# A second level of the seven-product form inside two of seven half products (batches 3 to 7)

## The chip, the core and the metric

The kernel runs on one core of a Trainium2 chip. The metric is the device time of one execution in microseconds. The core's engines work in parallel, each through its own queue in order: TensorE (PE; its weight loads, PEld, overlap its matmuls), VectorE (DVE), ScalarE (ACT), GpSimd (POOL) and SyncE (SP, which here only issues transfers). Semaphores order the engines among each other.

## The reference

Eight batches of 8 heads; `x` has 512 tokens of 64 per head, `state` 32 slots. Attention runs in both directions and its result, 544 rows of 512 per batch, goes through a feed-forward layer:

```python
scores = scale * np.matmul(x, state.transpose(0, 1, 3, 2))
...
xread = np.matmul(a, state)
...
sread = np.matmul(a2, x)
...
h = x @ w_in
g = h * (1.0 / (1.0 + np.exp(-h)))
return (g @ w_out).astype(np.float32)
```

`w_in` is 512x2048, `w_out` 2048x512. The output is 4352x512 in fp32.

## The kernel before

The order of instructions on each engine is written out by hand; the program keeps it.

**First layer.** Because `xread` is a product with the small state, the kernel multiplies state and `w_in` first (`w1_mms`, line 473; W1 is evicted by ACT and DVE in `w1_out`, lines 160 and 162). For a batch, the first layer is then 16 tiles ("slots" 0 to 15). Tile j takes two matmuls of 512 columns (line 540, `h <- aT, W`) into one of two PSUM banks (`psH`), and ACT's SILU (line 568) takes it from there into `g`. `upto(k)` issues tiles up to number k. The last 32 rows of each batch (`sread`) are gathered as a ninth, smaller batch, with tiles of four 256-column matmuls (line 558).

**Softmax of the next batch.** `scores_t` (line 336, also into the `psH` banks) and `exps_t` make the exponentials, transposed by a DMA (`e <- eT`, line 352). `norm_t(n)` sums them on DVE (line 363), takes the reciprocal (364), multiplies one half on POOL and one on DVE (366), and SP issues the transpose of the result, `aT <- an` (line 370). All first-layer tiles of batch n read `aT`.

**Second layer.** `g` (512 tokens, 2048 deep) times `w_out` (512 columns) is done in the seven-product form: tokens, depth and columns are halved, and class `Unit` (its products in `mm`, line 646) issues seven products instead of eight. One product is 8 steps of depth times 2 token blocks, 16 matmuls of 256 columns. Product 1 uses the first token half of `g`'s first depth half and block B11 of `w_out`; product 7 the sum `sums3` (DVE, line 591), made in place, and the weight sum D3. Products 1, 6 and 5 add up in one PSUM bank, `al` (bank "o1"), read in between by ACT (`keep`). Products 7, 2, 4 and 3 each start anew in bank "o0" (`be`), so each waits until DVE has read the one before. `kept[0]` and `kept[1]` are SBUF copies (DVE, line 162) of products 1 and 7. `sums2`, `sums1` and `sums4` are the other sums of `g`, on DVE, for products 6, 5 and 3. POOL and DVE add the parts into `o_sb` (line 594), and SP stores them.

**Order in a batch.** The loop over slots 5 to 15 (`for j in range(lead, NFT)`) issues a tile and then, through `early(j)`, a few units of products 1 and 7 from the list `todo`; one unit is one step of depth, two matmuls. `sums3` is issued at slots 5 and 9, `norm_t(n)` at slot 9, `sums2` from slot 13. After slot 15 come `group_a` (W1 pieces of a later batch, `scores_t`, and in batches 1, 4 and 6 `sread`), product 2 and its sum, then 6, 4, `group_b` (more W1 pieces), 5 with tile 0 of the next batch behind it, and 3 with tiles 1 to 4 of the next batch between its steps (`leads`). W1 pieces take PSUM banks in turn from four (`bank`, a0 to a3). `spread_x` (DVE) copies rows of x beside ones for `sread`. In batch 7 `place_xm` (DVE) arranges the gathered rows, and the tiles of the ninth batch are issued between the products.

Of the kernel before, what the change touches and what calls it, by code (L numbers as in the profile page):

```python
# [8 lines left out]
FP32 = mybir.dt.float32  # L9
# [9 lines left out]
B = 8  # L19
# [23 lines left out]
def kernel(  # L43
# [22 lines left out]
    opool = ctx.enter_context(tc.tile_pool(name="opool", bufs=1))  # L66
    o1pool = ctx.enter_context(tc.tile_pool(name="o1pool", bufs=1))
    spool = ctx.enter_context(tc.tile_pool(name="spool", bufs=1))
# [21 lines left out]
    w_out_sb = pers.tile([128, NFT, DM], BF16)  # L90
    wt = pers.tile([128, 4, 8, 256], BF16)
    xs = pers.tile([128, B, 128], BF16)
    xmT = pers.tile([128, 2, 4, NS, 4], BF16)
# [502 lines left out]
    def t_weights(which, k0, n, eng=nc.vector):  # L596
        k = ds(k0, n)
        for w in which:
# [6 lines left out]
            else:  # L605
                sub(eng, D4[:, k], B21[:, k], D2[:, k])

    class Unit:
        def __init__(self, b):
            self.b = b  # L610
            self.lo, self.hi = gh[b, 0], None
            self.s1 = spool.tile([128, 8, 256], BF16, tag="s1", name="s1")
            self.s2 = spool.tile([128, 8, 256], BF16, tag="s2", name="s2")
            self.al = psO.tile([128, 2, 256], FP32, tag="o1", name="o")
            self.be = None
            self.o = [
                opool.tile([128, 2, DM], FP32, tag=f"o_sb{i}", name="o_sb") for i in range(2)
            ]
# [40 lines left out]
        def sums2(self, k0, n):  # L659
            k = ds(k0, n)  # L660
            sub(nc.vector, self.s2[:, k], self.hi[:, k, 256:512], self.lo[:, k, 256:512])

        def sums1(self):
            for k0 in (0, 4):
                k = ds(k0, 4)
                add(nc.vector, self.s1[:, k], self.s2[:, k], self.lo[:, k, 0:256])

        def sums4(self):
            for k0 in (0, 4):
                k = ds(k0, 4)  # L670
                sub(nc.vector, self.hi[:, k, 0:256], self.hi[:, k, 0:256], self.s2[:, k])

        def block(self, i, c):
# [7 lines left out]
    def store(b, tt, eng):  # L681
        if b < B:
            if tt < 2:
                o_two[tt] = opool.tile([128, 2, DM], FP32, tag=f"o_sb{tt}", name="o_sb")
            o = o_two[tt % 2][:, tt // 2]
        else:
            o = o1pool.tile([128, DM], FP32, tag="o_one", name="o_sb")
        copy(eng, o[:], outs[tt][:])
        if b < B:
            nc.sync.dma_start(out_re[ds(136 * b, 128), tt, :], o)  # L690
        else:
            nc.sync.dma_start(out_sread[ds(512, 32), ds(4 * tt, 4), :], o[:])


    def sread_out_product():
# [4 lines left out]
        s1, s2 = t8("s1"), t8("s2")  # L700
        u1, u3 = (spool.tile([128, 256], FP32, tag=nm, name=nm) for nm in ("u1", "u3"))
        o = [o1pool.tile([128, DM], FP32, tag=f"o_s{i}", name="o_s") for i in range(2)]
        al = psO.tile([128, 256], FP32, tag="o1", name="o")
# [30 lines left out]
        add(nc.vector, s1[:], s2[:], a11)  # L734
        copy(nc.scalar, u1[:], al[:])
        p4 = product(a22, D4)
        add(nc.vector, u1[:], u1[:], o[1][:, hi])
        sub(nc.vector, s2[:], a12, s2[:])
        add(nc.vector, o[1][:, lo], u1[:], p4[:])
        product(s1, D1, al, False)  # L740
        copy(nc.scalar, u3[:], al[:])
        add(nc.vector, o[1][:, hi], o[1][:, hi], u3[:])
        out(1, 0, 512, nc.sync)
# [163 lines left out]
    for b in range(1, B):  # L907
# [82 lines left out]
        if n == B:  # L990
            upto(NFT * B + 2)
        if b == 1:
# [31 lines left out]
        units(6)  # L1024
        u.keep(nc.scalar, 1, 0)
# [75 lines left out]
```

## Time and profile before

| | us |
|---|---|
| median of 3 runs | 203.26 (203.02 to 203.26) |
| the profiled execution | 202.72 |
| its span | 200.9 |
| PE busy on first-layer tiles (line 540) | 72.7 |
| PE busy on the second layer (line 646) | 109.0 |
| ACT busy on SILU (line 568) | 79.9 |
| POOL busy, all its work | 72.3 |

The span is the time between the first and the last instruction in the profile. A row of the timeline has the start in us from the span's beginning, the duration in us, the engine, the source line, the operation, output and input, the shape and a count; in brackets stands the idle time before it and what ended it. Matmuls overlap at their ends, so the start of the next one tells more of their pace than their durations.

### The profile page before, as it was taken

How to read it: one execution, taken by the hardware profiler on the slowest of the kernel's cores; microseconds unless marked ns; L12 is line 12 of the kernel's file. 1: busy time of each engine (PE TensorE's matmuls, PEld its weight loads, DVE VectorE, ACT ScalarE, POOL GpSimd, SP SyncE). 2: the span in 40 equal slices, each digit the busy share in tenths (PEclk: the TensorE clock that was granted, in tenths of full speed). 3: DMA queues.
4: the chain of work that ended last, by engine and by line, in shares of the span. 5: the costliest groups of instructions: out<-in, count | busy, mean ns of one | idle time of the engine just before them, and what ended most of it. 6: DMA issues, size and time to landing. Idle time of an engine off the chain costs nothing.

```text
span 200.9 us, 4650 instructions
## 1 busy us (share of the span) xinstructions
PE 194.4 (97%) x1912; PEld 130.5 (65%) x1912; DVE 139.3 (69%) x244; ACT 138.3 (69%) x245; POOL 72.3 (36%) x89
## 2 busy tenths in 40 slices
PE   7799999999999999999999999999999999999992
PEld 2444435467766676667766676668666876688881
DVE  2852756989997899388938974779369955872072
ACT  2885657889767887778787957888588167724530
POOL 8674333795535602730373034323202230002200
PEclk9999999999999999999999999999999999999999
DMA  5999999993056995594239912943142005000232
GB/s 193 197 206 207 256 253 353 240 233 86 5 162 181 245 267 111 209 279 90 52 151 200 230 32 55 256 102 30 37 197 55 13 3 209 0 3 0 84 128 104
DMA packets 40821, 28.71 MB, mean 143 GB/s; under 512 B 27360, under 2 KB 37472, under 8 KB 40800
## 3 DMA queue, kind: packets, MB, share of 16 engines
q1 hardware_dynamic: 34592, 20.52, 39.8%
q0 software_dynamic: 5920, 7.64, 18.3%
q8 instruction: 15, 0.25, 0.5%
q10 hardware_dynamic: 288, 0.26, 0.4%
q14 instruction: 6, 0.05, 0.1%
HBM read 17.43 MB, written 8.91 MB: 131 GB/s over the span
## 4 chain that ended last, share of the span: by engine, by line
PE 93%; DMA 4%; DVE 0%; POOL 0%; ACT 0%; issue 0%; POOLq 0%
PE o L646 43%; PE h L540 27%; PE ps_w L473 5%; DMA w_in_sb<-in_moe_w_in_dram 4%; PE h L558 4%; PE o L577 3%; PE o_a L577 3%; PE o_s L709 2%; PE o L709 1%; PE ps_sr L420 1%; PE ps_scT L336 1%; PE ps_busy L168 1%; PE h L522 1%; PE ps_xt L257 1%; PE ps_at L402 1%; PE ps_sc L310 0%
## 5 line engine op out<-in xcount | busy, mean ns | idle before, releaser
L568 ACT ACTIVATE g<-h 128x512 bf16<-128x512 f32 (+1 forms) x142 | 79.9, 573 | 34.5 <-PE h L540 23.7
L646 PEld LDWEIGHTS <-g 128*128 128x128 bf16 x560 | 54.2, 98 | 29.2 <-issue 0.5
L540 PE MATMUL h<-aT,W 128*128 128x512 bf16 x252 | 72.7, 379 | 0.2 <-ACT W L160 0.2
L646 PE MATMUL o<-w_out_sb,g 128*128 128x256 bf16 x336 | 48.6, 273 | 0.0
L646 PE MATMUL o<-wt,g 128*128 128x256 bf16 x224 | 33.0, 273 | 0.0
L594 POOL TENSOR_TENSOR o_sb<-o_sb,kept 128x512 f32<-128x512 f32 x7 | 11.0, 1568 | 54.8 <-ACT o_sb L160 39.6
L540 PEld LDWEIGHTS <-W 128*128 128x128 bf16 x252 | 24.4, 98 | 8.7 <-issue 0.9
L646 PE MATMUL o<-wt,s 128*128 128x256 bf16 x224 | 27.4, 273 | 0.0
L594 DVE TENSOR_TENSOR o_sb<-o_sb,o 128x512 f32<-128x512 f32 x14 | 9.6, 683 | 23.9 <-PE o L646 20.5
L162 DVE CAST W<-ps_w 128x512 bf16<-128x512 f32 (+1 forms) x35 | 21.8, 666 | 6.1 <-PE ps_w L473 5.9
L646 PEld LDWEIGHTS <-s 128*128 128x128 bf16 x224 | 21.5, 98 | 4.4 <-issue 2.0
L160 ACT ACTIVATE W<-ps_w 128x512 bf16<-128x512 f32 (+1 forms) x31 | 16.4, 583 | 5.3 <-PE ps_w L473 5.2
L591 DVE TENSOR_TENSOR g<-g 128x1024 bf16<-128x1024 bf16 x15 | 11.6, 775 | 9.1 <-ACT g L568 9.0
L162 POOL CAST x_nat<-x_f 128x512 bf16<-128x512 f32 x24 | 15.8, 700 | 5.4 <-issue 3.9
L594 POOL TENSOR_TENSOR o_sb<-kept,o_sb 128x512 f32<-128x512 f32 x7 | 8.9, 1268 | 23.9 <-ACT o_sb L160 23.9
L160 ACT ACTIVATE o_sb<-o 128x512 f32<-128x512 f32 x15 | 8.9, 595 | 9.8 <-issue 6.6
L591 DVE TENSOR_TENSOR g<-g,s 128x1024 bf16<-128x1024 bf16 x14 | 13.7, 1019 | 0.0
L366 POOL TENSOR_TENSOR an<-e,rcn 128x512 bf16<-128x512 bf16 x5 | 7.7, 1540 | 16.1 <-DVE rcn L364 15.6
L162 DVE COPY kept<-o 128x512 f32<-128x512 f32 x14 | 9.6, 686 | 4.2 <-PE o L646 4.1
L591 DVE TENSOR_TENSOR s<-g 128x512 bf16<-128x512 bf16 (+3 forms) x23 | 12.0, 550 | 0.1
L577 PEld LDWEIGHTS <-g 128*128 128x128 bf16 x64 | 5.8, 98 | 7.0 <-issue 0.8
L473 PE MATMUL ps_w<-w_in_sb,stT 64*32 64x512 bf16 (+1 forms) x264 | 10.2, 375 | 0.1
(106 smaller groups left out, 214.7 us busy)
## 6 DMA issues: line engine op xcount, KB each, us to landing
out_dram<-o_sb SPq DMA_DIRECT2D x14, 512.0 KB, 2.7
x_f<-in_x_dram SPq DMA_DIRECT2D x6, 512.0 KB, 4.8
x_f<-in_x_dram POOLq DMA_DIRECT2D x2, 1024.0 KB, 11.4
x_f<-in_x_dram SPq DMA_DIRECT2D x2, 1024.0 KB, 6.5
w_out_sb<-in_moe_w_out_dram POOLq DMA_DIRECT2D x6, 256.0 KB, 11.3
w_in_sb<-in_moe_w_in_dram POOLq DMA_DIRECT2D x3, 512.0 KB, 10.5
x_f<-in_x_dram POOLq DMA_DIRECT2D x2, 512.0 KB, 14.5
out_dram<-o_sb SPq DMA_DIRECT2D x4, 256.0 KB, 5.5
```

The lines of the kernel that those rows point to most:

```text
L160: nc.scalar.activation(dst, src, func=COPY, bias=0.0)
L162: eng.tensor_copy(dst, src)
L366: eng.tensor_tensor(a[:, hg], e2[b][:, hg], rc[:, hg].to_broadcast([128, 4, 4, NS]), op=MULT)
L473: nc.tensor.matmul(pss[f, hg][ds(32 * s, 32), 0:n], stT[ds(r, 64), b, h // 2, s % 2, :], w_in_sb[ds(r, 64), h // 2, ds(f, n)], start=True, ...
L540: nc.tensor.matmul(h_ps[k][:], W1[b][:, hg, ds(128 * ft, 128)], aT[b][:, hg, :, :], start=(hg == 0), stop=(hg == 1), skip_group_check=True,)
L558: nc.tensor.matmul(ps[:, 0:256], w_in_sb[:, kt, ds(128 * ft, 128)], xmT[:, :, kt].rearrange("p t n b -> p t (n b)"), start=(kt == 0), stop ...
L568: nc.scalar.activation(gt[k], ps[:, 0:n], func=SILU, bias=0.0)
L577: nc.tensor.matmul(outs[tt][:], gt[b * NFT + ft][:, ds(128 * tt, 128)], w_out_sb[:, ft, :], start=(ft == 0), stop=(ft == NFT - 1), skip_gr ...
L591: eng.tensor_tensor(dst, a, c, op=SUB)
L594: eng.tensor_tensor(dst, a, c, op=ADD)
L646: nc.tensor.matmul(to[:, t, :], left[:, ds(128 * t, 128)], right[:, k, :], start=first and t == 0, stop=(k == 7), skip_group_check=True,)
L709: nc.tensor.matmul(to[:, 0:n], left[:, k], right[:, k, ds(c, n)], start=(first and k == 0), stop=(k == 7), skip_group_check=True,)
```

## The change

Product 7 of batches 3 to 7 and product 1 of batches 5 to 7 are each computed by seven inner products of their own: 128 tokens, 4 steps of depth, 128 columns. An inner product is four matmuls of 128 columns (`inner_mm`, line 736 of the changed kernel), 28 for the seven; it is now the unit of `todo`. Four sums of `g` are made for each on DVE (`inner_sums`), and four sums of weights once for all batches on POOL (`inner_weights`, in batch 2 for product 7 and in batch 4 for product 1, into the new tile `wt2`). Inner products 1, 6 and 5 add up in a new PSUM tile, `chain` (one half for each outer product), which DVE copies after each of the three; the other four have a quarter each of `al` or `be`. After inner product 5, DVE adds everything into `kept`. Since product 1 then lies only in `kept[0]`, ACT copies it back into `al` before product 6 adds to it. The inner sums share the SBUF places of `s1` and `s2`.

Moved with it: in batches 3 to 6 `norm_t(n)` goes from slot 9 to behind the sum of product 2; `spread_x` of batches 3, 4 and 5, and 6 and 7, goes to behind `group_b` of batches 2, 3 and 5; half of `place_xm` goes to POOL; in batch 7 three tiles of the ninth batch stand before product 2 instead of two. The tiles of the last product (`sread_out_product`) take other SBUF places; an unused branch of `store` is gone.

```diff
+    wt2 = pers.tile([128, 2, 4, 4, 128], BF16)
...
+    def inner_weights(p, eng):
+        d = [wt2[:, p == 7, i] for i in range(4)]
+        right = B11 if p == 1 else D3
+        y = {
+            (e, c): right[:, ds(4 * e, 4), ds(128 * c, 128)] for e in range(2) for c in range(2)
+        }
+        sub(eng, d[0], y[0, 1], y[0, 0])
+        sub(eng, d[1], y[1, 1], d[0])
+        sub(eng, d[2], y[1, 1], y[0, 1])
+        sub(eng, d[3], y[1, 0], d[1])
+
+    INNER = {3: (7,), 4: (7,), 5: (1, 7), 6: (1, 7), 7: (1, 7)}
...
-            self.s1 = spool.tile([128, 8, 256], BF16, tag="s1", name="s1")
-            self.s2 = spool.tile([128, 8, 256], BF16, tag="s2", name="s2")
+            self.s1 = self.s2 = None
...
             sub(nc.vector, self.s2[:, k], self.hi[:, k, 256:512], self.lo[:, k, 256:512])
 
         def sums1(self):
+            self.s1 = spool.tile([128, 8, 256], BF16, tag="s1", name="s1")
...
+        def quarters(self, p):
+            left = self.lo[:, :, ds(0 if p == 1 else 256, 256)]
+            right = B11 if p == 1 else D3
+            part = lambda a: {
+                (e, c): a[:, ds(4 * e, 4), ds(128 * c, 128)] for e in range(2) for c in range(2)
+            }
+            return part(left), part(right)
+
+        def inner_sums(self, p, which):
+            x, _ = self.quarters(p)
+            if p not in self.inner:
+                self.inner[p] = spool.tile(
+                    [128, 4, 4, 128], BF16, tag="s2" if p == 1 else "s1", name="inner"
+                )
+            t = [self.inner[p][:, i] for i in range(4)]
+            for i in which:
+                if i == 1:
+                    add(nc.vector, t[0], x[0, 1], x[1, 1])
+                elif i == 2:
+                    sub(nc.vector, t[1], t[0], x[0, 0])
+                elif i == 3:
+                    sub(nc.vector, t[2], x[0, 0], x[0, 1])
+                else:
+                    sub(nc.vector, t[3], x[1, 0], t[1])
+
+        def inner_mm(self, p, i):
+            x, y = self.quarters(p)
+            t = self.inner.get(p)
+            d = wt2[:, p == 7]
+            if self.chain is None:
+                self.chain = bank([128, 2, 128], FP32, "o_ch")
+            if p == 7 and self.be is None:
+                self.be = psO.tile([128, 2, 256], FP32, tag="o0", name="o")
+            q = (self.al if p == 1 else self.be).rearrange("p t (c n) -> p (t c) n", c=2)
+            ch = self.chain[:, int(p == 7)]
+            left, right, to, where = {
+                1: lambda: (x[0, 0], y[0, 0], ch, "ch"),
+                2: lambda: (x[1, 0], y[1, 0], q[:, 0], p),
+                3: lambda: (t[:, 3], y[1, 1], q[:, 2], p),
+                4: lambda: (x[1, 1], d[:, 3], q[:, 1], p),
+                5: lambda: (t[:, 0], d[:, 0], ch, "ch"),
+                6: lambda: (t[:, 1], d[:, 1], ch, "ch"),
+                7: lambda: (t[:, 2], d[:, 2], q[:, 3], p),
+            }[i]()
+            for k in range(4):
+                nc.tensor.matmul(
+                    to,
+                    left[:, k],
+                    right[:, k],
+                    start=where not in self.begun,
+                    stop=(k == 3),
+                    skip_group_check=True,
+                )
+                self.begun.add(where)
+            kept = self.kept[int(p == 7)]
+            if i == 1:
+                copy(nc.vector, kept[:, 0, 0:128], ch)
+            elif i == 6:
+                copy(nc.vector, kept[:, 1, 0:128], ch)
+            elif i == 5:
+                first = kept[:, :, 0:128]
+                u3 = spool.tile([128, 1, 128], FP32, tag="inner_u3", name="inner_u3")
+                copy(nc.vector, u3[:, 0], ch)
+                add(
+                    nc.vector,
+                    kept[:, :, 128:256],
+                    q[:, 2:4],
+                    u3.to_broadcast([128, 2, 128]),
+                )
+                add(nc.vector, first, first, q[:, 0:2])
+                add(nc.vector, kept[:, 1, 0:128], kept[:, 1, 0:128], q[:, 3])
...
+        both_u = xpool.tile([128, 4, 256], FP32, tag="x_nat", name="u")
+        u1, u3 = both_u[:, 0], both_u[:, 1]
+        o = [spool.tile([128, DM], FP32, tag=f"kept{i}", name="o_s") for i in range(2)]
...
-        last = 6 if b < 3 else 8
-        todo = [(1, k) for k in range(last)] + [(7, k) for k in range(8)]
-        todo += [(1, k) for k in range(last, 8)]
+        inner = INNER.get(b, ())
+        if 1 in inner:
+            todo = [(1, 1, 5), (1, 7, 7), (7, 1, 8), (1, 2, 9), (1, 4, 9), (7, 2, 10), (7, 4, 10)]
+            todo += [(1, 6, 11), (1, 3, 11), (7, 7, 11), (1, 5, 12), (7, 6, 12), (7, 3, 12)]
+            todo += [(7, 5, 13)]
+        elif inner:
+            todo = [(1, k - 8, k + 2) for k in range(7)] + [(7, 1, 9), (1, -1, 9)]
+            todo += [(7, 2, 10), (7, 4, 10), (7, 7, 11), (7, 6, 12), (7, 3, 12), (7, 5, 13)]
+        else:
+            last = 6 if b < 3 else 8
+            todo = [(1, k - 8, k + 2) for k in range(last)]
+            todo += [(7, k - 8, k + 4) for k in range(8)]
+            todo += [(1, k - 8, k + 2) for k in range(last, 8)]
         n_todo = len(todo)
 
         def unit():
-            p, k = todo.pop(0)
-            u.mm(p, k)
-            if (p, k) == (1, 7):
-                copy(nc.vector, u.kept[0][:], u.al[:])
-            if (p, k) == (7, 7):
-                copy(nc.vector, u.kept[1][:], u.be[:])
+            p, k, _ = todo.pop(0)
+            if k > 0:
+                u.inner_mm(p, k)
+                return
+            u.mm(p, k + 8)
+            if k == -1:
+                copy(
+                    nc.vector,
+                    u.kept[int(p == 7)][:],
+                    (u.al if p == 1 else u.be)[:],
+                )
...
-                and todo[0][1] + (0 if todo[0][0] == 1 else 2) <= j - 2
-                and (n_todo - len(todo)) * (NFT - lead) < 16 * (j + 1 - lead)
+                and todo[0][2] <= j
+                and (n_todo - len(todo)) * (NFT - lead - bool(inner)) < n_todo * (j + 1 - lead)
...
                 u.sums3(0, 4)
+                for p in inner:
+                    u.inner_sums(p, (3,))
...
+                for p in inner:
+                    u.inner_sums(p, (1, 2, 4))
...
-                    norm_t(n)
-                    if b in SREAD_AT:
-                        spread_x(n)
+                    if not inner:
+                        norm_t(n)
                 else:
                     for half in range(2):
-                        place_xm(half, nc.vector)
+                        place_xm(half, (nc.vector, nc.gpsimd)[half])
...
-            upto(NFT * B + 2)
+            upto(NFT * B + 3)
...
+        if 1 in inner:
+            copy(nc.scalar, u.al[:], u.kept[0][:])
         add(nc.vector, u.block(0, 0), u.kept[0][:], u.be[:])
+        if inner and n < B:
+            norm_t(n)
...
-                    upto(NFT * B + 2 + (step + 1) * (NFT - 2) // 26)
+                    upto(NFT * B + 3 + (step + 1) * (NFT - 3) // 26)
...
+        if b == 2 or b == 4:
+            inner_weights({2: 7, 4: 1}[b], nc.gpsimd)
...
-            if n < B and b not in SREAD_AT:
-                spread_x(n)
...
+        for i in {2: (3,), 3: (4, 5), 5: (6, 7)}.get(b, ()):
+            spread_x(i)
```

More of the change, by code (lines that the diff above doesn't have):

```diff
@@ L66 @@
     opool = ctx.enter_context(tc.tile_pool(name="opool", bufs=1))
-    o1pool = ctx.enter_context(tc.tile_pool(name="o1pool", bufs=1))
     spool = ctx.enter_context(tc.tile_pool(name="spool", bufs=1))
@@ L611, in __init__ @@
             self.lo, self.hi = gh[b, 0], None
-            self.s1 = spool.tile([128, 8, 256], BF16, tag="s1", name="s1")
-            self.s2 = spool.tile([128, 8, 256], BF16, tag="s2", name="s2")
+            self.s1 = self.s2 = None
             self.al = psO.tile([128, 2, 256], FP32, tag="o1", name="o")
             self.be = None
+            self.chain = None
+            self.inner = {}
+            self.begun = set()
             self.o = [
@@ L660, in sums2 @@
             k = ds(k0, n)
+            if k0 == 0:
+                self.s2 = spool.tile([128, 8, 256], BF16, tag="s2", name="s2")
             sub(nc.vector, self.s2[:, k], self.hi[:, k, 256:512], self.lo[:, k, 256:512])
         def sums1(self):
+            self.s1 = spool.tile([128, 8, 256], BF16, tag="s1", name="s1")
             for k0 in (0, 4):
@@ L681, in store @@
     def store(b, tt, eng):
[L682 to L687, printed above, removed]
+        if tt < 2:
+            o_two[tt] = opool.tile([128, 2, DM], FP32, tag=f"o_sb{tt}", name="o_sb")
+        o = o_two[tt % 2][:, tt // 2]
         copy(eng, o[:], outs[tt][:])
[L689 to L692, printed above, removed]
+        nc.sync.dma_start(out_re[ds(136 * b, 128), tt, :], o)
     def sread_out_product():
@@ L700, in sread_out_product @@
         s1, s2 = t8("s1"), t8("s2")
-        u1, u3 = (spool.tile([128, 256], FP32, tag=nm, name=nm) for nm in ("u1", "u3"))
-        o = [o1pool.tile([128, DM], FP32, tag=f"o_s{i}", name="o_s") for i in range(2)]
+        both_u = xpool.tile([128, 4, 256], FP32, tag="x_nat", name="u")
+        u1, u3 = both_u[:, 0], both_u[:, 1]
+        o = [spool.tile([128, DM], FP32, tag=f"kept{i}", name="o_s") for i in range(2)]
         al = psO.tile([128, 256], FP32, tag="o1", name="o")
@@ L734, in sread_out_product @@
         add(nc.vector, s1[:], s2[:], a11)
-        copy(nc.scalar, u1[:], al[:])
+        copy(nc.scalar, u1, al[:])
         p4 = product(a22, D4)
-        add(nc.vector, u1[:], u1[:], o[1][:, hi])
+        add(nc.vector, u1, u1, o[1][:, hi])
         sub(nc.vector, s2[:], a12, s2[:])
-        add(nc.vector, o[1][:, lo], u1[:], p4[:])
+        add(nc.vector, o[1][:, lo], u1, p4[:])
         product(s1, D1, al, False)
-        copy(nc.scalar, u3[:], al[:])
-        add(nc.vector, o[1][:, hi], o[1][:, hi], u3[:])
+        copy(nc.scalar, u3, al[:])
+        add(nc.vector, o[1][:, hi], o[1][:, hi], u3)
         out(1, 0, 512, nc.sync)
```

## The prediction

> **What bounds the kernel now.** I read the page first (busy shares, chain), then the timeline of one batch on all engines, the source view of the softmax transpose, the groups with shapes kept apart, and the timeline of the last products.
>
> ```profile
> PE 194.4 (97%) x1912; PEld 130.5 (65%) x1912; DVE 139.3 (69%) x244; ACT 138.3 (69%) x245; POOL 72.3 (36%) x89
> ...
> PE 93%; DMA 4%; DVE 0%; POOL 0%; ACT 0%; issue 0%; POOLq 0%
> ```
>
> TensorE sets the time almost alone, so a microsecond in which its queue waits is a microsecond of the kernel. What the other engines do is free only until something in PE's queue waits for it. How much room there is shows in batch 5:
>
> ```profile
> 124.99 1.03 PE L540 MATMUL h<-aT,W 128*128 128x512 bf16 x4
> 125.62 1.08 ACT L568 ACTIVATE g<-h 128x512 bf16<-128x512 f32 x2 [0.27 <-PE h L540]
> 126.29 0.59 PE L540 MATMUL h<-aT,W 128*128 128x512 bf16 x2
> ...
> 128.81 1.21 DVE L363 TENSOR_REDUCE rs<-e 128x32 f32<-128x1024 bf16 x1
> 130.05 0.35 DVE L364 RECIPROCAL rcn<-rs 128x32 f32<-128x32 f32 x1
> 130.49 1.55 POOL L366 TENSOR_TENSOR an<-e,rcn 128x512 bf16<-128x512 bf16 x1 [3.22 <-DVE rcn L364]
> 132.06 1.23 SPq L370 DMA_TRANSPOSE aT<-an  x1
> 133.01 0.59 PE L540 MATMUL h<-aT,W 128*128 128x512 bf16 x2
> 134.19 0.50 PE L336 MATMUL ps_scT<-xT,stT 64*32 64x512 bf16 x8
> 134.63 1.92 PE L646 MATMUL o<-w_out_sb,g 128*128 128x256 bf16 x16
> 136.59 0.69 DVE L594 TENSOR_TENSOR o_sb<-kept,o 128x512 f32<-128x512 f32 x1 [0.17 <-PE o L646]
> ...
> 141.62 0.59 PE L540 MATMUL h<-aT,W 128*128 128x512 bf16 x2
> 142.06 0.60 PE L646 MATMUL o<-w_out_sb,g 128*128 128x256 bf16 x4
> ```
>
> The reader is to see four things. The softmax of the next batch (128.81 to the transpose issued at 132.06) ends long before its first user, the first-layer tile at 141.62. Product 2 starts at 134.63 and its sum follows at 136.59, 1.96 later. First-layer tiles stand no closer than two in 1.30 (124.99, then 126.29, two banks later, when the first SILU of the pair at 125.62 has ended). The last tile (133.01) is followed by product 2 after 1.62, because the score matmuls wait for its SILU. I set a batch's clock to zero at its tile 5 (125.42 here, the second pair of the x4 row). Product 2 then starts at 9.21 and product 3 at 16.64; in batches 3, 4, 6, 7 the same rows give 9.21, 10.09, 9.51, 9.30 for product 2 and 17.51, 18.39, 17.61 for product 3 of batches 3, 4, 6.
>
> **What the inner form saves.** Eight half products (five sevenths, three firsts) go from 16 matmuls of 256 columns to 28 of 128. The tail has both widths with a weight load before each:
>
> ```profile
> 195.02 0.86 PEld L709 LDWEIGHTS <-g 128*128 128x128 bf16 x8
> 195.13 1.04 PE L709 MATMUL o_s<-w_out_sb,g 128*128 128x256 bf16 x8
> 195.89 0.99 PEld L709 LDWEIGHTS <-s 128*128 128x128 bf16 x16
> 196.00 1.06 PE L709 MATMUL o_s<-w_out_sb,s 128*128 128x128 bf16 x16
> ```
>
> Eight wide ones take 0.87 (195.13 to 196.00), 109 ns each; sixteen narrow ones 1.06 with one pipe tail of 0.22, so 0.84/15 = 56 ns each. 16 x 109 = 1.74 against 28 x 56 = 1.57: 0.17 saved, eight times 1.4 us. From above the narrow pace is bounded by the load row, 98 ns.
>
> The Trainium skill speaks against this: "TensorE: Matmul & The Clock Gate", section "Back-to-back issue gap", puts a sustained stream of load and matmul pairs at about 81 ns for 128 columns. The row above shows 56 over sixteen, so I go by the row; by the page the 224 narrow matmuls would cost 5.6 us more than I take.
>
> **What it adds on DVE and POOL.** Sizes come from these groups:
>
> ```profile
> L591 POOL TENSOR_TENSOR wt<-w_out_sb,wt 128x1024 bf16<-128x1024 bf16 x2 | 4.3, 2165 | 0.2
> ...
> L591 DVE TENSOR_TENSOR s<-g 128x512 bf16<-128x512 bf16 x14 | 5.2, 416 | 0.0
> L162 DVE COPY xmT<-xs 64x256 bf16<-64x256 bf16 x8 | 3.0, 375 | 0.1
> L594 DVE TENSOR_TENSOR o_s<-u,o_s 128x128 f32<-128x128 f32 x2 | 0.6, 290 | 0.2 <-PE o_s L709 0.2
> ```
>
> Per inner product DVE gets four sums of 128x512 (0.42 each, 0.45 when one needs the last), and instead of one 0.69 copy two 128x128 copies (0.29), a copy of 0.29, two 128x256 sums (0.42) and one of 0.29. The last four are a chain of 1.40. In the built order the chain bank makes PE wait: inner product 5 for the copy after 6, the seventh's 6 for the copy after the first's 5, the seventh's 5 for the copy after its 6; product 2 waits for the whole last chain, since both use bank "o0".
>
> Batch 5, on its clock. Slots 6 and 7 now have 0.22 between tiles where 1.30 per two tiles is needed: tile 9 comes 0.38 late. SILU 7 ends at 2.6, DVE copies the seventh's product 1 (to 3.28), takes the second third sum (0.69) and six inner sums: done at 6.34. The copy after the first's product 6 stands behind them, to 6.55; so its product 5 starts at 6.6 where PE was ready at 6.09. The seventh's 6 then at 7.37, its 5 at 8.69, the last tile at 8.92 (7.59 before). DVE does the second-half sum (0.69), then the last chain, 9.17 to 10.57. Product 2 starts at 10.7, not 9.21: +1.5, the 0.35 saved already in it. Batch 6 has the same queue: 10.7, not 9.51. In batch 7 four copies of 0.375 stand before that copy too, so product 5 starts at 8.15 and product 2 at 12.2; one more 0.43 tile is moved ahead of it, so +2.5. In batches 3 and 4 only the seventh is inner, the chain is done at 9.24, and the last tile stays at 7.64, against 7.59: the saving ends in the wait for its SILU, +0.1.
>
> **What the moved softmax costs.** In batches 3 to 6 the reduction now follows product 2's sum on DVE. After product 2's start: 1.96, sum to the next start 0.60, reduction 1.24, reciprocal 0.39, POOL 1.55, then the transpose, whose landing this view gives:
>
> ```profile
> DMA to landing us min/median/max: 3.0/3.6/6.2
> ```
>
> 5.74 + 3.0 = 8.75 at the least. PE arrives at 6.98 (141.62 - 134.63; 7.87, 7.87 and 7.67 in batches 3, 4, 6, with W matmuls). SP holds nothing late ahead of it; behind it wait the e transpose and the stores, which have room. On DVE the reduction's 2.3 us also push the sums for products 5 and 3 back, and POOL at work slows those: the two subtractions ahead of product 3 took 2.36 at 139.00 beside POOL's add and 1.28 at 179.67 without. So product 3 starts: batch 3 at 18.6 to 19.2 (+1.45 mid); batch 5 at 19.9 to 20.6 (+3.65, with the 1.5 above); batch 6, where the sread reciprocals hold product 2's sum to 14.1, at 20.9 to 21.5 (+3.6). In batch 4 POOL does four inner weight subtractions between the softmax and the o_sb add, at 2.165/2 = 1.1 each: softmax to 15.9, weights to 20.4, add 21.7, DVE's add 22.4; product 3 needs its bank and starts at 22.55, not 18.39: +4.15. That is POOL undisturbed; its product beside a DVE product takes 1.55 (above), alone 1.04 (line 386's group), so four DVE sums between the four subtractions would add 0.5 to 0.6 each: up to +6.4. I take the middle, +5.2, since some of the four will fall elsewhere. The same subtractions in batch 2 end before POOL's next add at 75.2, which hides them; uncovered they would cost 4.4. The moved row copies fall into DVE's idle 2 to 3 us after the W casts: nothing, 1.5 if that gap is gone. The tail moves tiles, not their number.
>
> **Sum.** 1.45 + 5.2 + 3.65 + 3.6 + 2.5 = 16.4 on the profiled 202.72 (span 200.9 and 1.8 around it): 219.1. The median of the runs is 0.54 above that execution; this lies within the range. Own range: with landing 3.0, POOL undisturbed and batch 7 at +2.0, 1.15 + 4.15 + 3.3 + 3.3 + 2.0 = 13.9; with landing 3.6, POOL at its worst and batch 7 at +3.0, 1.75 + 6.4 + 4.0 + 3.9 + 3.0 = 19.05; so 216.6 to 221.8.
>
> **Rivals.** (1) The chain hides and only softmax and POOL bite: tiles 9 to 15 would have to leave DVE a microsecond that I don't see. For it: DVE idles 1.3 to 1.7 us in these slots before. Batches 3 to 7 then cost about 1.3 + 4.15 (POOL undisturbed) + 1.8 (8.75 - 6.98) + 2.0 - 0.35 = 8.9: 211.6. (2) The narrow stream costs more, at the 98 ns load: 224 x 42 ns = 9.4, half of it hidden in slots that wait anyway; 4.7 on top gives 223.8. Against it: the tail. A falling clock would look alike: the page shows PEclk 9 in every slice, but also no PE pause over 1 us after the start, and batch 4 gets one of nearly 3. The skill's page named above ("Why this matters for your kernels") warns of pauses over about 3 us; nothing here shows it. (3) The other side, faster: the transposed softmax is there before PE. It decides at 7.0 us after product 2's start; then only 1.4 is left, 201.3. For it: PE's columns do shrink. Against it: five durations in a row that end at 8.75. That the inner form doesn't save at all is in (2).
>
> **Chances.** Forecast 0.65, (1) 0.17, (2) 0.13, (3) 0.05. Predicted 219.1; the range 211.5 to 223.5 reaches to (1) and close to (2). A measurement tells 0.2% (0.4 us) from no change: faster 0.04, same 0.01, slower 0.95.
>
> **What would show it.** Right: PE idle before line 540 at the start of batches 4 to 7, released by the aT transpose; idle of about 2 us before product 3 of batch 4, led back to POOL's wt2; short idles before line 736 released by DVE's copies of o_ch; PE matmul time on line 736 spaced 56 ns. Wrong: no idle at the batch starts, or line 736 spaced near 98.

## The result, and the profile after

The changed kernel takes 223.34 us, the median of four runs (222.62 to 225.82), beside 203.14 for the kernel before on the same chip: a ratio of 1.1023 with a 95% interval of 1.0935 to 1.111. The profiled execution took 223.41, its span is 221.6 against 200.9 (+20.7). The direction was as predicted, the size was not: 219.1 was forecast, and the time lies beyond the upper end of the forecast's own range (221.8) and at the very end of its wide one (223.5: the median lies just inside, the ratio on the 203.26 of the kernel before gives 224.05). Of the four executions of the run e10 below two, the profiled one among them, were slow (over 1.5% longer than its fastest), and its ratio is that of the other two.

The page of the changed kernel: busy shares, the chain that ended last, and the groups of the second layer.

```profile
PE 198.4 (90%) x1990; PEld 130.8 (59%) x2008; DVE 166.2 (75%) x312; ACT 139.4 (63%) x248; POOL 86.8 (39%) x101
...
PE 65%; DVE 20%; DMA 9%; issue 2%; ACT 1%; POOL 1%; DVEq 0%; POOLq 0%
...
L661 PE MATMUL o<-w_out_sb,g 128*128 128x256 bf16 x288 | 42.0, 277 | 6.4 <-DVE o_sb L594 6.0
L661 PE MATMUL o<-wt,s 128*128 128x256 bf16 x224 | 28.0, 273 | 5.0 <-DVE s L594 5.0
...
L594 DVE TENSOR_TENSOR s<-s,g 128x1024 bf16<-128x1024 bf16 x15 | 17.2, 1186 | 0.0
```

PE had 93% of the chain and now has 65%; DVE, which had none, has 20%. PE waits 6.0 us for sums in `o_sb` and 5.0 for the `s` sums, which take 1.19 us each. The reader should keep "DVE `s`" in mind: the forecast expected PE to stand before line 540, released by `aT`.

To see where the time went, I split each batch by three rows of its timeline. The *front* runs from the four-matmul row of line 540 (tiles 4 and 5) to the start of product 6, the *middle* from there to the start of product 3, the *close* from there to the next batch's four-matmul row.

| us | fronts, batches 4, 5, 6, 7 | middles, 3, 4, 5, 6 | closes, 3, 4, 5, 6 |
|---|---|---|---|
| before | 12.28, 11.39, 11.70, 11.48 | 6.54, 6.55, 5.68, 6.34 | 3.05, 3.05, 3.04, 3.04 |
| after | 12.33, 12.81, 12.83, 14.75 | 8.11, 12.26, 8.10, 8.97 | 3.20, 4.63, 3.04, 3.04 |

The middles lost 12.3 us, the fronts 5.9 (0.43 of it the ninth batch's tile that batch 7 now has ahead of product 2, given back in the tail), the closes 1.7. About 1.1 came up before batch 3.

Batch 5 shows a middle (timeline of the changed kernel, several engines):

```profile
148.23 0.69 DVE L594 TENSOR_TENSOR o_sb<-kept,o 128x512 f32<-128x512 f32 x1
148.83 1.21 DVE L363 TENSOR_REDUCE rs<-e 128x32 f32<-128x1024 bf16 x1
...
150.51 1.55 POOL L366 TENSOR_TENSOR an<-e,rcn 128x512 bf16<-128x512 bf16 x1 [17.25 <-DVE rcn L364]
...
151.08 3.21 DVE L594 TENSOR_TENSOR s<-s,g 128x1024 bf16<-128x1024 bf16 x2
...
152.03 1.71 POOL L594 TENSOR_TENSOR o_sb<-o_sb,kept 128x512 f32<-128x512 f32 x1
152.09 1.23 SPq L370 DMA_TRANSPOSE aT<-an  x1
...
152.67 1.05 PE L661 MATMUL o<-wt,s 128*128 128x256 bf16 x8 [0.99 <-DVE s L594]
...
154.34 1.05 PE L661 MATMUL o<-wt,s 128*128 128x256 bf16 x8 [0.62 <-DVE s L594]
...
155.22 0.38 PE L540 MATMUL h<-aT,W 128*128 128x512 bf16 x1
...
156.13 0.60 PE L661 MATMUL o<-w_out_sb,g 128*128 128x256 bf16 x4 [0.53 <-DVE o_sb L594]
```

The softmax (148.83 on) stands ahead of the `s` sums in DVE's queue, and the two sums take 3.21 us where such a pair takes 1.28 in e6 below: each ends some 0.6 us, its own length, after an instruction of POOL's has ended (152.06 and 153.74), as if it could begin only then. Both halves of product 5 wait for their sum (152.67, 154.34), then product 3 for the `o_sb` add further down in DVE's queue. With a landing of 3.0 us (an estimate from the shortest landing that the prediction shows), `aT` is there at 155.1, and tile 0 starts at 155.22 without a wait shown.

Batch 4 is the largest single loss (same view, and the table of stretches with the granted clock as the third number from the end):

```profile
122.33 1.60 POOL L591 TENSOR_TENSOR wt<-w_out_sb 128x512 bf16<-128x512 bf16 x1
...
124.00 1.48 POOL L591 TENSOR_TENSOR wt<-w_out_sb,wt 128x512 bf16<-128x512 bf16 x1
...
125.45 1.59 POOL L591 TENSOR_TENSOR wt<-w_out_sb 128x512 bf16<-128x512 bf16 x1
...
127.00 1.59 POOL L591 TENSOR_TENSOR wt<-w_out_sb,wt 128x512 bf16<-128x512 bf16 x1
128.56 1.26 POOL L594 TENSOR_TENSOR o_sb<-o_sb,kept 128x512 f32<-128x512 f32 x1
...
130.59 1.01 PE L661 MATMUL o<-w_out_sb,g 128*128 128x256 bf16 x4 [4.54 <-DVE o_sb L594]
...
131.40 1.06 PE L540 MATMUL h<-aT,W 128*128 128x512 bf16 x2
...
132.25 1.06 PE L661 MATMUL o<-w_out_sb,g 128*128 128x256 bf16 x4
```

```profile
128.00:130.60 2.60, 0.01 (x1) 0.01 (x1) 0.75 (x2) 0.00 (x0) 2.60 (x3) 0.97 0.00 0
130.60:133.20 2.60, 2.60 (x11) 1.51 (x11) 1.73 (x3) 0.60 (x1) 2.60 (x5) 0.50 0.49 202
```

POOL's four weight subtractions take 1.5 to 1.6 us each and hold its add back to 128.56; PE stands 4.54 us. Then it runs at a granted clock of 0.50, which lasts from 130.45 to 133.87: the line-540 pair at 131.40 takes 0.85 to the next row (132.25), where 0.43 is usual. That is the 1.6 us of the close of batch 4.

### The profile page after: what moved, and what is told of

It is laid out like the page before. It is cut to its first block, busy times and chain, and to the rows that moved or that the text cites. A ratio compares the mean times of both kernels' runs of the same rounds, so it can differ in the third digit from the quotient of the medians.

```text
span 221.6 us, 4909 instructions
## 1 busy us (share of the span) xinstructions
PE 198.4 (90%) x1990; PEld 130.8 (59%) x2008; DVE 166.2 (75%) x312; ACT 139.4 (63%) x248; POOL 86.8 (39%) x101
## 4 chain that ended last, share of the span: by engine, by line
PE 65%; DVE 20%; DMA 9%; issue 2%; ACT 1%; POOL 1%; DVEq 0%; POOLq 0%
PE o L661 25%; PE h L540 18%; DVE s L594 4%; DVE g L591 3%; PE h L558 3%; DMA w_in_sb<-in_moe_w_in_dram 3%; DMA xT<-x_nat 3%; PE o_a L577 3%; PE o L577 3%; PE ps_w L473 3%; DVE inner L591 2%; PE o_ch L736 2%; DVE stT L162 2%; DMA e<-eT 2%; DVE o_sb L594 2%
## 5 line engine op out<-in xcount | busy, mean ns | idle before, releaser
L540 PE MATMUL h<-aT,W 128*128 128x512 bf16 x237 | 70.2, 383 | 0.4 <-ACT W L160 0.2
L661 PEld LDWEIGHTS <-g 128*128 128x128 bf16 x432 | 42.1, 98 | 25.4 <-issue 7.4
L661 PE MATMUL o<-w_out_sb,g 128*128 128x256 bf16 x288 | 42.0, 277 | 6.4 <-DVE o_sb L594 6.0
L661 PE MATMUL o<-wt,s 128*128 128x256 bf16 x224 | 28.0, 273 | 5.0 <-DVE s L594 5.0
L540 PEld LDWEIGHTS <-W 128*128 128x128 bf16 x252 | 23.1, 98 | 10.5 <-issue 2.4
L661 PEld LDWEIGHTS <-s 128*128 128x128 bf16 x224 | 21.1, 98 | 10.9 <-DVE s L594 7.9
L594 POOL TENSOR_TENSOR o_sb<-o_sb,kept 128x512 f32<-128x512 f32 x7 | 10.7, 1527 | 22.5 <-DVE g L591 16.1
L661 PE MATMUL o<-wt,g 128*128 128x256 bf16 x144 | 19.3, 273 | 0.1
L162 POOL CAST x_nat<-x_f 128x512 bf16<-128x512 f32 x24 | 16.7, 734 | 6.4 <-issue 4.2
L594 POOL TENSOR_TENSOR o_sb<-kept,o_sb 128x512 f32<-128x512 f32 x7 | 9.5, 1358 | 20.9 <-ACT o_sb L160 17.6
L594 DVE TENSOR_TENSOR s<-s,g 128x1024 bf16<-128x1024 bf16 x15 | 17.2, 1186 | 0.0
L160 ACT ACTIVATE o_sb<-o 128x512 f32<-128x512 f32 x15 | 8.9, 595 | 10.7 <-PE o L661 6.2
L736 PEld LDWEIGHTS <-inner 128*128 128x128 bf16 x128 | 8.9, 97 | 9.9 <-issue 5.0
L591 DVE TENSOR_TENSOR g<-g,s 128x1024 bf16<-128x1024 bf16 x14 | 12.2, 913 | 0.0
```

The source lines that it names most:

```text
L160: nc.scalar.activation(dst, src, func=COPY, bias=0.0)
L162: eng.tensor_copy(dst, src)
L540: nc.tensor.matmul(h_ps[k][:], W1[b][:, hg, ds(128 * ft, 128)], aT[b][:, hg, :, :], start=(hg == 0), stop=(hg == 1), skip_group_check=True,)
L591: eng.tensor_tensor(dst, a, c, op=SUB)
L594: eng.tensor_tensor(dst, a, c, op=ADD)
L661: nc.tensor.matmul(to[:, t, :], left[:, ds(128 * t, 128)], right[:, k, :], start=first and t == 0, stop=(k == 7), skip_group_check=True,)
```

## The experiments

Times are medians, ratios with 95% intervals; the kernel before, run beside them, took 203.5 us (e1 to e4), 203.2 (e5 to e9), 203.1 (e10 to e12) and 203.2 (e13). A difference from the changed kernel is one between medians; by the ratios it comes out up to 1.5 us larger, and both are given where it matters. The rows below each name give fronts, middles and closes as above, where they matter.

**The kernel before with the softmax moved** (e4).

```diff
                 elif n < B:
-                    norm_t(n)
+                    if b < 3:
+                        norm_t(n)
...
         add(nc.vector, u.block(0, 0), u.kept[0][:], u.be[:])
+        if 2 < b and n < B:
+            norm_t(n)
```

> The kernel before with one thing changed: norm_t of batches 3 to 6 moved from tile 9 to behind product 2's o_sb add, as the change does it; no inner products. Theory (the move alone costs 1.5 in batch 3, 1.6 in 4, 2.4 in 5 and 2.1 in 6): about 210.7, up 7.6, with a range of 5 to 9. Rival (without the inner products DVE is free by product 2 and the moved softmax is hidden behind products 2 and 6): up by less than 2 us.

212.55 us, 1.0423 [1.0368, 1.0479]: up 9.1. Fronts as before (12.29, 11.41, 11.71, 11.48), middles 8.72, 8.11, 8.71, 8.67. The move costs 9 us with no inner product in the kernel, at the upper end of the theory's range.

**The changed kernel with the softmax back at tile 9** (e3).

```diff
                 elif n < B:
-                    if not inner:
-                        norm_t(n)
+                    norm_t(n)
...
-        if inner and n < B:
-            norm_t(n)
```

> The changed kernel with the softmax of the next batch (norm_t) back at tile 9 in batches 3 to 6, where the kernel before has it; the seven-product form inside the halves stays as changed. Theory (the move of the softmax costs 1.5 to 2.4 us in each of batches 3 to 6 and helps hold POOL's subtractions up in batch 4, the longer chain on DVE gets about 1 us of it back): about 216.5, down 7, with a range of 5 to 9. Rival (the chain of DVE copies and sums for the inner products is the cost, the place of the softmax is not): down by less than 2 us, or slower than the changed kernel, with product 2 of batches 5 and 6 beyond 12.5 us.

218.41 us, 1.0714 [1.0645, 1.0783]: down 4.9 by the medians and 6.3 by the ratios, at the lower end of the theory's range and far from the rival's 2. Middles 6.55, 7.95, 5.67, 6.40, nearly as before (batch 4 keeps 1.4 from POOL); but fronts 13.21, 16.69, 15.06, 15.03. The softmax now stands between the inner sums and the copy out of the chain bank (timeline of this kernel, batch 5):

```profile
136.71 0.42 DVE L591 TENSOR_TENSOR inner<-g,inner 128x512 bf16<-128x512 bf16 x1
137.05 1.21 DVE L363 TENSOR_REDUCE rs<-e 128x32 f32<-128x1024 bf16 x1
...
139.29 0.28 DVE L162 COPY kept<-o_ch 128x128 f32<-128x128 f32 x1
```

```profile
139.62 0.59 PE L736 MATMUL o_ch<-wt,inner 128*128 128x128 bf16 x4 [2.64 <-DVE kept L162]
```

PE stands 2.64 us where it stood 0.40 in the changed kernel, and some of batch 5's front is a slow clock behind that wait (0.50 from 139.65 to 143.07). The two costs are not a sum: the move takes 7.3 us out of the fronts and puts 10.9 into the middles.

**Sevenths only, at either place of the softmax** (e5 with it at tile 9, e13 with it moved).

```diff
-    INNER = {3: (7,), 4: (7,), 5: (1, 7), 6: (1, 7), 7: (1, 7)}
+    INNER = {b: (7,) for b in range(3, 8)}
...
-        if b == 2 or b == 4:
-            inner_weights({2: 7, 4: 1}[b], nc.gpsimd)
+        if b == 2:
+            inner_weights(7, nc.gpsimd)
```

> The changed kernel with the inner form in the seventh half products only (batches 3 to 7; the first ones whole as before) and the softmax back at tile 9. Read against the run with both halves and the softmax at tile 9 (218.4): there batch 4, which has the seventh alone, had a front (tile 5 to product 6) 0.9 us over the kernel before, and batches 5 to 7, which have both, 5.3, 3.4 and 3.6 over. Theory (the copies out of the first's chain, which stand on DVE behind six inner sums and the softmax, are the large part): some 0.9 us a batch, about 208 (206.5 to 209.5). Rival (each inner half costs the same): about 212.

> The changed kernel with the inner form in the seventh half products only (batches 3 to 7), the softmax behind product 2 as the change has it, and so no weight subtractions of POOL's in batch 4. It completes the square of softmax place and inner form. Theory (the move costs 9 us whatever stands in the front; the sevenths alone, with the softmax out of their way, cost the fronts of batches 4 to 7 nothing; the firsts cost the rest, through their chain on DVE, their weights and the clock): middles 8.1 to 9 us in batches 3 to 6, fronts 12.3, 11.4 to 11.7, 11.7 to 12 and 11.9, about 213.2 (212 to 214.5). Rival (each inner half costs its share in the front also with the softmax gone): fronts of batches 5 to 7 up by 0.6 or more each, and 215 or above.

206.82 us, 1.0178 [1.0143, 1.0212], and 212.0 us, 1.0448 [1.0416, 1.0479]. Fronts of e5: 13.14, 12.28, 12.34, 12.04; of e13: 12.32, 11.47, 11.52, 12.02. Both times lie at the lower ends of their theories' ranges. With the softmax out of their way the sevenths cost the fronts nothing (batch 7 has its extra 0.43); beside it, 0.6 to 0.9 each in batches 4 to 6. The square, as microseconds over the kernel before:

| | softmax at tile 9 | moved |
|---|---|---|
| no inner form | 0 | 9.1 |
| sevenths | 3.6 | 8.8 |
| sevenths and firsts | 14.9 | 20.2 |

The firsts, with their weights and the clock, carry 11.3 to 11.4 in either column (10.9 and 11.7 by the ratios).

**What holds PE in the middles** (e6, e10, both on the kernel before with the softmax moved). In e6 DVE multiplies both halves; in e10 the softmax stands behind the `s` sums too. The first edit is shown against e4; of the second only the new place is shown.

```diff
-            norm_t(n)
+            norm_t(n, (nc.vector, nc.vector))
```

```diff
             u.sums1()
+            if 2 < b and n < B:
+                norm_t(n)
```

> The kernel before with the softmax moved behind product 2 (212.6) and, besides, the scaled half that POOL multiplies (1.55 us beside DVE's s sums) put on DVE (another 0.6). Theory (PE waits for DVE's s sums, which stand behind the softmax and each of which waits for an instruction of POOL's to end, 3.2 us for two instead of 1.3): about 208 (206.5 to 209.5), the middle of batch 5 (product 6 to product 3) down from 8.7 to about 7.3. Rival (what holds PE is the transposed softmax, aT, landing 3 us after its issue, as the prediction had it): aT is issued at about the same moment, so within 1 us of 212.6.

> The kernel before with the softmax of batches 3 to 6 moved one step further than the change moves it, behind DVE's s sums for product 5 as well; no inner products. The s sums then run as early as in the kernel before. Theory A (PE waits for the s sums alone; aT has room): the middles (product 6 to product 3) go back to about 6.5, 6.5, 5.7 and 6.3 us, about 204.5 (203 to 206). Theory B (the landing of aT lies close behind the s sums, and takes their place when they are early): the softmax begins about 1.3 us later, aT lands about 1.5 us later, PE's wait goes to L540 released by aT, and the time is 212.5 or above (212 to 216).

e6: 212.36 us, 1.0455 [1.0419, 1.0491], as the rival had it, but not by its reason alone. Its batch 5:

```profile
143.18 2.36 DVE L366 TENSOR_TENSOR an<-e,rcn 128x512 bf16<-128x512 bf16 x2
145.46 1.28 DVE L594 TENSOR_TENSOR s<-s,g 128x1024 bf16<-128x1024 bf16 x2
```

```profile
146.19 1.92 PE L646 MATMUL o<-wt,s 128*128 128x256 bf16 x16 [1.80 <-DVE s L594]
148.91 0.38 PE L540 MATMUL h<-aT,W 128*128 128x512 bf16 x1 [0.80 <-DMA aT<-an]
```

The `s` sums are fast again, but now the second multiplication ahead of them ends 0.55 us after POOL's add (143.41 to 144.99); PE still waits for `s`, and then for `aT`, which was issued later (4.86 us after the start of product 6, 4.05 in e4). This run did not separate the two. e10 did: ratio 1.0705 [1.0601, 1.0808], 217.4 us by it. Batch 3:

```profile
102.25 0.61 PE L540 MATMUL h<-aT,W 128*128 128x512 bf16 x2 [2.24 <-DMA aT<-an]
```

No wait for `s` is left; PE stands 2.24, 2.33, 3.22 and 2.88 us for `aT` in batches 3 to 6, and the middles are 8.97, 9.06, 9.43 and 9.75. Theory B in kind: whichever of the two waits is eased, the other stands. The time is beyond B's 216, and here too the clock is in it: the closes are 4.71, 3.04, 5.57 and 4.03 where 3.04 is usual.

**The softmax one batch earlier** (e9 on the kernel before, e8 on the changed one, there with POOL's subtractions split two and two; neither makes it at its old place any more).

```diff
             group_b()
+        if 1 < b and m < B:
+            norm_t(m)
```

> The kernel before with the softmax of batches 4 to 7 made one batch earlier, in DVE's wait for product 3; nothing else. Theory (softmax in the front is hidden behind SILU's pace, so taking it out gains nothing, and DVE has the room for it there): 203.4 within 0.7. Rivals: the front is bound by DVE too, then down by 1 to 2 us; or the new place delays POOL's o_sb add and the casts behind it, then up by 1 us or more.

> The changed kernel, inner form in both halves, with the softmax of batches 4 to 7 made one batch earlier, in the 3.4 us in which DVE waits for product 3, and POOL's four weight subtractions split, two behind the o_sb add of batch 3, two behind that of batch 4. Theory (the middles, from product 6 to product 3, are late through the softmax and the subtractions alone, and the fronts, from tile 5 to product 6, through the inner form's chain on DVE): middles of batches 3 to 6 back at 6.5, 6.5, 5.7 and 6.3 us (within 0.5), fronts 1.4, 1.1 and 3.3 over the kernel before in batches 5 to 7 as in the changed kernel, about 210 (208.5 to 212). Rival (the middles are held by the inner form itself): 216 or more.

e9: 204.52 us, 1.0059 [1.0034, 1.0084]. Taking 2.2 us of DVE's work out of the fronts leaves those of batches 5 and 6 at 11.40 and 11.70 (batch 7, which makes no softmax, at 11.48): DVE does not bound them. That part held; but the time is up 1.3 us, beyond the theory's 0.7, and 0.9 of it is the front of batch 4 (13.18), where PE stands 1.01 us for the transposed x (issued at 108.61, when POOL's casts have ended; in the kernel before at 105.41), as the second rival had it in kind. e8: 220.0 us, 1.082 [1.0784, 1.0856], neither theory's number. The middles are back to 6.55, 6.55, 5.67 and 6.40, so the inner form itself does not hold them. But the fronts are 15.37, 19.19, 13.89 and 15.04, in the worst of them, batch 5, for a reason I had not foreseen (timeline of DVE):

```profile
128.66 1.22 DVE L363 TENSOR_REDUCE rs<-e 128x32 f32<-128x1024 bf16 x1 [1.64 <-DMA e<-eT]
...
133.15 0.69 DVE L594 TENSOR_TENSOR o_sb<-o_sb,o 128x512 f32<-128x512 f32 x1 [2.16 <-POOL o_sb L594]
```

In batch 4 the softmax waits for its own input, POOL's add for the softmax, DVE for POOL, and PE 4.09 us for the inner sums of batch 5. That is that placing's fault, so this run says nothing of the fronts.

**POOL's subtractions in batch 4** (e2: behind the `o_sb` add in POOL's queue; e11: at the end of batch 3, so that they run in the front).

```diff
-        if b == 2 or b == 4:
-            inner_weights({2: 7, 4: 1}[b], nc.gpsimd)
+        if b == 2:
+            inner_weights(7, nc.gpsimd)
         units(6)
         u.keep(nc.scalar, 1, 0)
         add(nc.gpsimd, u.block(1, 0), u.block(1, 0), u.kept[1][:])
+        if b == 4:
+            inner_weights(1, nc.gpsimd)
```

```diff
             transpose_x(m + 1)
+        if b == 3:
+            inner_weights(1, nc.gpsimd)
```

> The changed kernel with POOL's four weight subtractions of batch 4 issued behind its o_sb add instead of ahead of it. Theory (they cost batch 4 about 4 us of its 5.8 and, through the pause, 1.6 of clock): product 3 of batch 4 starts about 20 us after the batch's fifth tile's zero instead of 24.15, the clock doesn't fall, and the time is about 217.8 (down 5.5). Rival (the moved softmax delays the o_sb add just as long, and the subtractions ran in time that was lost anyway): product 3 stays beyond 22.5 and the time falls by less than 2.5 us.

> The changed kernel with POOL's four weight subtractions of batch 4 issued at the end of batch 3, so that they run in the front of batch 4, where POOL stands still for 11 us. Theory (behind product 2 they hold up DVE's sums for products 5 and 3 and POOL's o_sb add together, wherever in POOL's queue they stand there; in the front they hold up little): the middle of batch 4 falls from 12.3 us to about 8.1, as in batches 3 and 5, the front of batch 4 grows by less than 1, and the clock's fall of 1.6 us is gone from batch 4; about 218.2 (217 to 219.5). Rival (they slow DVE in the front by as much as they did behind product 2): 221 or more.

e2: 221.94 us, 1.0881 [1.0817, 1.0945], down 1.4 by the medians and 2.9 by the ratios: nearer the rival's size than the theory's 5.5. The middle of batch 4 is 10.02 instead of 12.26, which puts product 3 at 21.9 on the batch's clock, between the two theories, and its close is 4.88, with the slow clock still in it. The subtractions run beside DVE's `g` sums, as before, and these still take 3.2 us a pair; DVE no longer waits for POOL's add (2.26 us in the changed kernel), but it comes late to its own `o_sb` add by itself. e11: 220.14 us, 1.0831 [1.0788, 1.0875], between the two. The middle is 8.11 as forecast, but the front grew by 1.85 (14.18), and the clock's fall went from batch 4 to batch 6. So the subtractions cost batch 4 4.15 us ahead of POOL's add (12.26 against 8.11), 1.91 behind it (e2), and 1.85 in the front.

**The clock** (e1: 18 matmuls of zeros ahead of product 3 of batch 4).

```diff
+        if b == 4:
+            keep_busy(18, psO, "o1")
         units(3, {1: 2, 3: 3, 5: 4, 7: 5})
```

> The changed kernel with 18 matmuls of zeros (512 columns, about 3.9 us) put into the 4.5 us in which PE stands still before product 3 of batch 4; nothing else moves. Theory (the pause lets the granted clock fall, and the slow clock costs what follows): the granted clock stays at 1.0 after product 3 of batch 4, the L540 pairs behind it come every 0.43 us instead of every 0.85, and the time falls by about 1.6 us, from 223.3 to about 221.8. Rival (the slow pairs come from something that the matmuls of zeros don't touch, a queue or the DMAs behind them): the pairs stay at 0.85 and the time stays at 223.3 within 0.4, or rises.

222.81 us, 1.0921 [1.0853, 1.0989]. The mechanism is as the theory had it: the close of batch 4 is 3.04 us, pairs 0.43 apart:

```profile
127.20 4.04 PE L168 MATMUL ps_busy<-busy 128*128 128x512 bf16 x18 [1.39 <-ACT o_sb L160]
131.08 0.60 PE L661 MATMUL o<-w_out_sb,g 128*128 128x256 bf16 x4
131.52 0.59 PE L540 MATMUL h<-aT,W 128*128 128x512 bf16 x2
131.95 0.60 PE L661 MATMUL o<-w_out_sb,g 128*128 128x256 bf16 x4
```

But of 1.6 us only 0.5 shows in the median (2.1 by the ratios): the zeros overran the pause by 0.8 (middle 13.04), and in the profiled execution the clock fell later, behind the 1.82 us pause of batch 7 (front 16.02 instead of 14.75), to 0.50 from 193.33 on, 0.58 in the mean of this row:

```profile
193.00:195.00 2.00, 2.00 (x13) 1.05 (x11) 1.63 (x5) 1.19 (x2) 0.00 (x0) 0.58 0.00 0
```

Of the four executions, two had a mean clock of 1.00 (222.39 and 222.42 us), two of 0.99 (223.19 and 223.56).

**`place_xm` of batch 7 all on POOL** (e12).

```diff
-                        place_xm(half, (nc.vector, nc.gpsimd)[half])
+                        place_xm(half, nc.gpsimd)
```

> The changed kernel with all eight place_xm copies of batch 7 on POOL, none on DVE. Theory (the four DVE copies, 1.5 us, stand ahead of the copy out of the first's chain, and PE's 1.8 us wait in batch 7 is theirs): the front of batch 7 falls from 14.75 to about 13.3 us, the time from 223.3 to about 221.8. Rival (the wait comes from the six inner sums ahead of them): the front of batch 7 changes by less than 0.5.

222.3 us, 1.0962 [1.0906, 1.1017]. In the profiled execution PE's wait went from 1.82 to 0.40, so it was the copies'; but the front fell only from 14.75 to 14.21, because DVE's inner sums now run beside POOL's copies and grew (the first pair from 1.18 to 1.61 us, the next from 0.42 to 0.84), so that PE comes to the wait 0.9 us later. The cause is shown, the gain is a third of what the theory had.

No version here beats the kernel before.

## Why the prediction was wrong

The terms of the sum, on the clock that the prediction used:

| | predicted | measured |
|---|---|---|
| ahead of batch 3 | 0 | 1.10 |
| batch 3 | 1.45 | 1.64, and 0.15 behind product 3 |
| batch 4 | 5.2 | 5.76 |
| slow clock behind it | 0 | 1.59 |
| batch 5 | 3.65 | 3.83 |
| batch 6 | 3.6 | 3.75 |
| batch 7 | 2.5 | 2.84 |
| sum | 16.4 | 20.7 |

*The clock is the step that failed.* The prediction saw that batch 4 would get a pause of "nearly 3" us and that a falling clock would look like its rival (2), but it gave the sum a full clock after it. The pause was 4.54 and the clock 0.50 behind it, which cost 1.59, the largest of the terms by which the sum fell short; without it the measured terms come to 19.1, the upper end of the prediction's own range. e1 shows the link: with the pause filled, batch 4 runs at 1.0. So the warning of the Trainium skill ("TensorE: Matmul & The Clock Gate", section "Why this matters for your kernels", which advises against PE pauses over about 3 us) held here, where the kernel before could not show it. The runs go further than that sentence: the clock fell behind pauses of 1.82 (e1), 2.24 (e10) and 2.29 us (e2), and did not behind one of 1.82 (after) and one of 2.33 (e10).

What decides between these can be read from the traces. The granted clock changes only at moments that lie a whole number of 3.41 us apart: in the changed kernel it rises at 4.16, 37 such stretches before its fall at 130.45, and rises again one stretch later. Cut at these moments, the fourteen profiled executions have 821 stretches at full clock. In 11 of them PE stood still for 1.85 us or more, in one pause or in several, and behind each of the 11 the clock fell; in the other 810 it stood still for 1.83 us or less, and behind none of them did it fall. In e10 the pause of 2.24 us lies within one stretch, and that of 2.33 is divided between two (start and end, length, PE's busy time first; the clock is again the third number from the end):

```profile
99.75:103.16 3.41, 1.17 (x10) 0.63 (x8) 3.41 (x6) 0.35 (x2) 0.00 (x0) 1.00 0.40 77
123.64:127.05 3.41, 2.34 (x40) 1.48 (x16) 3.41 (x5) 1.75 (x4) 1.46 (x2) 1.00 0.80 119
127.05:130.47 3.42, 2.16 (x14) 1.39 (x15) 1.59 (x3) 1.51 (x3) 0.35 (x1) 1.00 0.19 37
```

e3 has two pauses of 2.64 us; the first lies in one stretch and the clock fell, the second is divided and it did not. So for a pause of this size it depends on its place among the stretches, which no change here controlled. This was sorted out of the traces afterwards; no run was made to test it.

*Batch 4* was mis-sized by 0.6. The mechanism was right, POOL's subtractions ahead of the `o_sb` add; one took 1.5 to 1.6 beside DVE, near the prediction's worst, where it took a middle. e2 adds what the prediction missed: with the subtractions behind the add, 1.91 of 4.15 us stay, since DVE's sums slow down beside them as well.

*Ahead of batch 3* nothing was forecast. Part is the execution's own: product 6 of batch 1 starts at 50.26 us, in e1, e2, e11 and e12, the same program up to there, at 49.87, 50.92, 49.53 and 49.59, in the kernel before at 49.72. From there to product 6 of batch 3 the changed kernel takes 44.43 against 43.80 (44.07 to 44.53 in those four), 0.07 of it in the front of batch 3. The four other kernels without the weight subtractions of batch 2 (e4, e6, e9, e10) take 43.91 to 43.95, and e13, which has them, 44.51. So 0.1 to 0.7 us come with these subtractions, which the prediction called hidden, or with the row copies moved into the same batch; no run took the two apart, and the cause is not shown.

*The moved softmax* was sized well (product 3 at 20.47 where 19.9 to 20.6 was said, 21.36 for 20.9 to 21.5), and e4 prices the move at 9.1 alone. But the wait was named wrongly: PE stood before product 5 for the `s` sums, not before line 540, where only weight loads waited for `aT`, 0.26 us in batch 3 and 0.36 in batch 4. By its own sign ("no idle at the batch starts") the prediction was wrong here. The size came out right by luck, because the two waits are nearly tied; e10, which frees the `s` sums, brings the forecast wait out.

*The chain on DVE* held: product 2 at 10.61, 10.63 and 12.57 for 10.7, 10.7 and 12.2, with the short idles before line 736 that were announced, and the copies of batch 7 as the cause of the last (e12). *The inner form* saves what was said, and it comes to nothing: eight inner matmuls take 0.61 us, less a pipe tail of 0.22 and over the seven steps between them 56 ns each (timeline, batch 7).

```profile
188.60 0.61 PE L736 MATMUL o<-wt,g 128*128 128x128 bf16 x8
```

Against the 81 ns that the Trainium skill's page named above gives under "Back-to-back issue gap" the row decides again. So the narrow stream in rival (2) did not happen; that its number, 223.8, came near is luck: the other reason that it named, the clock, is 1.6 of the 4.3 us by which the sum fell short. Rival (1), the chain that hides, is true of the sevenths alone (e13). Rival (3) falls with e4 and e10.

## What to carry to other kernels

Saving columns on PE is worth nothing in a stage that something else paces; e9 and e13 show that these fronts stay at 11.4 to 11.7 us whether DVE or PE is given room. Price a moved step against every wait behind it, not only against its own consumer: here two waits were tied, and easing one showed the other. And wherever the sum itself makes PE stand for some 2 us within a few microseconds, in one pause or in several, put the slow clock behind it into the sum, as a chance and with its price (1.6 us here), not into a rival.

## What the runs showed of the hardware

In the middles of batches 4 and 5 of the changed kernel a DVE sum of bf16 in SBUF (0.64 us) that met a POOL instruction ended some 0.6 us after that instruction had ended; three pairs of sums beside POOL took 3.1 to 3.2 us instead of 1.28. The granted clock fell to 0.50 for one stretch of 3.41 us or for two, through work and not only through the pause; eight times it came back after the first, in which PE stood still for 0.60 us or less, and three times (e8, e10, e12) it stayed for the second, with 0.88, 0.98 and 1.59 us of idle in the first. In e11 and e12 it fell in batch 6 behind two pauses of only 1.24 and 0.63 us, which lay in one stretch; the same two pauses in the changed kernel lay in two, and it did not.
